# First columns in six pieces, routing products twice an iteration, low parts of the weights on VectorE, raw words through GpSimd's queue

## The chip, the cores and the metric

The kernel runs on one core of one Trainium2 chip. The metric is the device time of one execution in microseconds (us). Five engines work side by side in the core: TensorE (PE in the profile; its weight loads are PEld), VectorE (DVE), ScalarE (ACT), GpSimd (POOL) and SyncE (SP, which here only issues transfers). Each of them takes its own instructions strictly in order. Transfers are issued from the queues of SP or of GpSimd and carried out by 16 DMA engines.

## What is computed

Attention over keys and values that are averaged in groups of eight; its output goes through a mixture of experts, one expert per token; that output goes through a dense layer with a maximum of three products.

```python
def _attn_ref(q, k, v):                      # 8 x 8 x 576 x 64
    k_p = k.reshape(B, H, Sp, pool, D).mean(axis=3)      # pool = 8
    v_p = v.reshape(B, H, Sp, pool, D).mean(axis=3)
    scores = scale * np.matmul(q, k_p.transpose(0, 1, 3, 2))
    attn = np.exp(scores - np.max(scores, axis=-1, keepdims=True))
    attn = attn / (np.sum(attn, axis=-1, keepdims=True) + 1e-09)
    return np.matmul(attn, v_p)

def _moe_ref(x, expert_emb, tau, w1, w2):    # x: 4608 x 512, 8 experts, F = 1024
    logits = xn @ en.T / tau                 # x and expert_emb with rows of length 1
    expert_idx = np.argmax(logits, axis=1)
    gate_w = probs[np.arange(N), expert_idx] # softmax of the logits
    for e in range(E):
        mask = expert_idx == e
        h = np.maximum(x[mask] @ w1[e], 0.0)
        out[mask] = gate_w[mask, None] * (h @ w2[e])
    return out

def _moe2_ref(x, w1, w2, w3, w_out):         # d_ff = 768
    h = np.maximum(np.maximum(x @ w1, x @ w2), x @ w3)
    return h @ w_out
```

## The kernel before

**Attention** (0 to about 212 us) goes over 36 tiles of 128 tokens in a loop `for it in range(NT + 4)`. An iteration does the scores of tile it-1 (`stage_s`), the product with the values of tile it-3 (`stage_a`), the transposes of the queries of tile it (`stage_q`) and the output of tile it-4 (`stage_x`). Between these stand the jobs that prepare the keys and values of a later batch b, from the list that `prep_steps(b)` returns; the table `at_` says in which iteration each job is written. For the six batches b = 2 to 7 the jobs are: GpSimd adds the groups of eight (`pool_k2` and `pool_v`, lines 267 and 278); ScalarE copies the pooled keys a second time beside themselves (`dup_k`), and GpSimd spreads the values into a block form (`spread_v`, line 284); TensorE transposes the keys (`trans_k`, tile ptk), then the values by themselves (`trans_v`, tile ptv, line 307); at last `vdot` multiplies the transposed values with the experts' vectors.

**Routing** runs on VectorE in the gaps. A routine queues generators of small steps; `fill(n)` takes n of them. A step that needs TensorE stops its generator, and `boundary()` moves such a stop on by one state each time that it is called: in one call the products are written, in a later one the steps behind them are released. The attention loop calls `boundary()` once, at the top of an iteration. One chain of such steps ends in the list `idg`, which says which tokens the first items of the experts take.

**The experts** (212 to 728 us): 18 items of 256 tokens and 4 of 128. `run` goes through eight steps per item, four products with w1 (`mm1`, tile ph) and four with w2 (`mm2`, tile py). Two steps ahead, `split(i, piece)` takes a piece of the raw weights to a high part (ScalarE, tile whi) and a low part (tile wlo, line 1001): on GpSimd for odd pieces of items 0 to 4 (`i < NE`, with NE = 5) and for the very first, otherwise on VectorE. `gather` fetches an item's tokens by `idg` through GpSimd's queue (tile xrow, line 961) and `transpose_x` turns them (tile px). ScalarE and VectorE make high and low parts of the hidden values (tiles hhi and hlo).

`between` is called twice in each of the eight steps. It first serves the rest of the routing, and after that two generators. `conversions` turns 48 blocks of 64-bit words of the dense layer's weights into floats on VectorE: a block's raw words (tile cvraw, 256 KB, two buffers) are loaded two blocks ahead (line 1134, SP's queue), and a block takes five steps (lines 1150, 1163, 1166, 1168 with the next load, 1171). `combinations` makes sums of these weights and stores them (line 1210, tile wst to wdram, GpSimd's queue), and ends with `columns(0, 1)`: the first token columns of the dense layer are read back from memory (tile yr, line 1249, SP's queue) in four pieces of 192, each in the one buffer that there is. After the load of a piece it lets three calls of `between` pass, and then writes the sums and the high and low parts (`sums`, lines 1266 to 1278, steps of one piece). From item 17 on (`last_pairs`) `between` moves this generator on twice.

**The dense layer** (728 us to the end) multiplies by a scheme of seven products (line 1579).

The order on each engine is the order in which the code writes the instructions. No scheduler stands between.

Of the kernel before, what the change touches and what calls it, by code (L numbers as in the profile page):

```python
# [21 lines left out]
def attention_moe_moe_kernel(  # L22
# [27 lines left out]
    P = 128  # L50
# [65 lines left out]
    if True:  # L116
# [61 lines left out]
        if True:  # L178
# [69 lines left out]
            def prep_steps(b):  # L248
# [3 lines left out]
                vp = qp.tile([P, 5, D], F32, tag="vp", name=f"vp{b}")  # L252
# [22 lines left out]
                def pool_v(c0, c1, n):  # L275
                    for w in (4, 2, 1):
                        dst = vt[0:n, c0:c1, 0:w, :] if w > 1 else vp[0:n, c0:c1, :].unsqueeze(2)
                        nc.gpsimd.tensor_tensor(dst, vt[0:n, c0:c1, 0:w, :], vt[0:n, c0:c1, w : 2 * w, :], op=A.add)
# [12 lines left out]
                def trans_k(cs, h0, h1):  # L291
# [9 lines left out]
                    nc.scalar.copy(kb[D:P, h0:h1, 1, :], ps[D:P, 0:col].rearrange("p (h s) -> p h s", s=SP))  # L301

# [35 lines left out]
                if b == 1:  # L338
                    pk = [lambda: (pool_k(0), pool_k(1)), lambda: (pool_k(2), pool_k(3)), lambda: pool_k(4)]
                    pk += [lambda: (pool_v(0, 4, P), pool_v(4, 5, 64))]  # L340
                else:
                    pk = [lambda: (pool_k2(), pool_v(0, 4, P), pool_v(4, 5, 64))]
# [650 lines left out]
            def split(i, piece):  # L993
                src = w_raw(piece)
                if not (i >= NPAIR and piece < 4):
# [4 lines left out]
                    eng = nc.gpsimd if i < NE and piece % 2 or (i, piece) == (0, 0) else nc.vector  # L1000
# [115 lines left out]
            def conversions():  # L1116
# [61 lines left out]
            def combinations():  # L1178
# [49 lines left out]
                for _ in columns(0, 1):  # L1228
                    yield
# [6 lines left out]
            def columns(g, bufs):  # L1236
# [5 lines left out]
                w_ = HW // 2 if bufs == 1 else HW  # L1242
                rows = []
                for c in range(2):
                    for n in range(0, HW, w_):
                        t = tl["yr"].tile([P, 2, 2, w_], F32, tag="yr", name=f"yr{g}_{c}_{n}", bufs=bufs)
# [3 lines left out]
                        if bufs == 1:  # L1250
                            for _ in range(3):
                                yield
                            yield from sums(t, c, n, w_)
                        rows.append((t, c, n, w_))
                if bufs > 1:
                    yield
                    for a_ in rows:
                        yield from sums(*a_)
# [61 lines left out]
            def between(half, p_=0):  # L1320
# [7 lines left out]
                else:  # L1328
# [3 lines left out]
                    if last_pairs:  # L1332
                        next(cb, None)
# [94 lines left out]
            for b in range(1, B):  # L1428
                need = (b // 2) * 9 + (0 if b % 2 == 0 else 4)
                at_ = [need - 7, need - 3, need - 1, need, need, need + 1, need + 2]  # L1430
                at_ = {1: [2, 3, 3, 2, 3, 4, 4, 5, 6, 7], 2: [need - 5, need - 2] + at_[2:]}.get(b, at_)
# [9 lines left out]
            for it in range(NT + 4):  # L1441
# [16 lines left out]
                while kvnext < B and kvnext * 4.5 - 11 <= it:  # L1458
                    kv[kvnext] = (load_rows("kraw", k, kvnext, KC), load_rows("vraw", v, kvnext, RC))
# [70 lines left out]
    def second(st, groups, again=False):  # L1530
# [143 lines left out]
        ahead = columns(groups[0], 2) if again else iter(())  # L1674
        for g in groups:
# [5 lines left out]
            ahead = columns(g + 1, 2) if nxt else iter(())  # L1681
# [83 lines left out]
```

## Time and profile before

| what | value |
|---|---|
| three runs | 1281.42, 1281.93, 1282.61 us (median 1281.93) |
| profiled execution | 1281.78 us, its span 1279.9 us |
| TensorE busy | 1225.6 us, 96% of the span |
| VectorE busy | 802.7 us, 63% |
| ScalarE busy | 581.4 us, 45% |
| GpSimd busy | 346.5 us, 27% |

Busy shares are averages over stages with different limits. How a stage stands is read from the table by windows further down; "PEclk" there is the granted TensorE clock, of which 1.00 is the higher level. A row of a timeline gives the start, the duration, engine, line, operation, tiles and shape; a bracket says how long the engine was idle before it and for what. "x4" behind a row says that four instructions follow each other there.

### The profile page before, as it was taken

The page shows a single profiled execution, that of the slowest core. Times are in us where ns is not written, and L with a number is a line of the kernel's source. Part 1 is how long each engine was busy: PE and PEld are TensorE (multiplying, and loading weights), DVE is VectorE, ACT ScalarE, POOL GpSimd, SP SyncE. Part 2 cuts the span into 40 slices and gives each one's busy share as a digit, 9 for nine tenths or more (in the row PEclk, how much of TensorE's full clock was granted, in tenths as well). Part 3 has the DMA queues.
Part 4 walks back from the last instruction along what each step waited for, and adds up shares of the span by engine and source line. Part 5 has one row for each costly group of instructions (what it writes and reads, how often), then busy time and mean ns, then how long its engine had stood idle before and what let it go on. Part 6 is the DMA issues. An engine that isn't in the chain of part 4 may idle for free. (4 is left out here: it accounts for less than half of the span.)

```text
span 1279.9 us, 22372 instructions
## 1 busy us (share of the span) xinstructions
PE 1225.6 (96%) x8281; PEld 1164.2 (91%) x8281; DVE 802.7 (63%) x1551; ACT 581.4 (45%) x1040; POOL 346.5 (27%) x357
## 2 busy tenths in 40 slices
PE   4999998989899999999989999999999999999997
PEld 3888787989899999999979899899998998998995
DVE  6776784788789899899654446355256345345450
ACT  2566555435566666666535423333234223223231
POOL 7985643434500403223000300201302103103101
PEclk9899999999999999999999999999999999999999
DMA  9867335421885644953516768367376475664631
GB/s 261 252 202 214 121 113 206 150 82 35 232 286 199 217 147 161 292 175 132 190 50 229 265 238 304 115 248 280 119 266 231 165 253 209 210 240 181 226 146 52
DMA packets 100088, 246.21 MB, mean 192 GB/s; under 512 B 17102, under 2 KB 57084, under 8 KB 91908
## 3 DMA queue, kind: packets, MB, share of 16 engines
q1 hardware_dynamic: 90660, 201.67, 47.3%
q0 software_dynamic: 9312, 43.04, 9.5%
q8 instruction: 67, 1.10, 0.3%
q14 instruction: 49, 0.40, 0.1%
HBM read 252.23 MB, written 46.98 MB: 234 GB/s over the span
## 5 line engine op out<-in xcount | busy, mean ns | idle before, releaser
L1579 PE MATMUL p<-yhi,wt 128*128 128x384 f32 x1512 | 387.2, 336 | 0.7 <-ACT yo L1093 0.7
L1579 PEld LDWEIGHTS p<-yhi,wt 128*128 128x128 f32 x1512 | 273.5, 188 | 1.4 <-ACT yo L1093 0.9
L1579 PE MATMUL p<-ylo,wt 128*128 128x384 f32 x756 | 254.0, 336 | 0.0
L1587 ACT COPY s<-p 128x384 f32<-128x384 f32 x162 | 77.8, 480 | 222.2 <-PE p L1579 214.0
L1021 PE MATMUL ph<-xhi,whi 128*128 128x256 f32 x576 | 164.9, 286 | 8.0 <-DVE hlo L1037 8.0
L1069 PE MATMUL py<-hhi,wlo 128*128 128x256 f32 x576 | 164.0, 285 | 3.3 <-DVE wlo L1001 3.3
L1069 PE MATMUL py<-hhi,whi 128*128 128x256 f32 x576 | 165.4, 287 | 1.0 <-ACT whi L999 1.0
L1021 PE MATMUL ph<-xhi,wlo 128*128 128x256 f32 x576 | 163.8, 284 | 1.9 <-DVE wlo L1001 1.9
L1021 PE MATMUL ph<-xlo,whi 128*128 128x256 f32 x576 | 163.7, 284 | 1.2 <-DVE xlo L988 1.2
L1069 PE MATMUL py<-hlo,whi 128*128 128x256 f32 x576 | 163.5, 284 | 0.0
L1579 PEld LDWEIGHTS p<-ylo,wt 128*128 128x128 f32 x756 | 142.1, 188 | 0.5
L1608 DVE TENSOR_TENSOR blk<-p,s 128x384 f32<-128x384 f32 x108 | 59.7, 553 | 114.1 <-PE p L1579 113.9
L1564 POOL DMA_INDIRECT gt<-gbuf,ix x26 | 37.1, 1428 | 322.4 <-DMA ix<-idbuf 316.0
L1021 PEld LDWEIGHTS ph<-xhi,whi 128*128 128x128 f32 x576 | 111.0, 193 | 9.6 <-DVE hlo L1037 9.2
L1069 PEld LDWEIGHTS py<-hhi,wlo 128*128 128x128 f32 x576 | 111.0, 193 | 4.1 <-DVE wlo L1001 4.1
L1021 PEld LDWEIGHTS ph<-xhi,wlo 128*128 128x128 f32 x576 | 111.2, 193 | 2.3 <-DVE wlo L1001 2.3
L1021 PEld LDWEIGHTS ph<-xlo,whi 128*128 128x128 f32 x576 | 111.1, 193 | 1.4 <-DVE xlo L988 1.4
L1069 PEld LDWEIGHTS py<-hhi,whi 128*128 128x128 f32 x576 | 111.1, 193 | 1.2 <-ACT whi L999 1.2
L1069 PEld LDWEIGHTS py<-hlo,whi 128*128 128x128 f32 x576 | 111.2, 193 | 0.0
L1001 DVE TENSOR_TENSOR wlo<-w2raw,whi 128x1024 fp32r<-128x1024 f32 x78 | 94.8, 1221 | 9.5 <-ACT whi L999 9.5
L961 POOL DMA_INDIRECT xrow<-xbuf,idg x40 | 69.6, 1740 | 113.4 <-PE px L982 87.8
L999 ACT CAST whi<-w2raw 128x1024 fp32r<-128x1024 f32 x88 | 91.8, 1044 | 5.5 <-PE py L1069 3.9
(307 smaller groups left out, 2338.0 us busy)
## 6 DMA issues: line engine op xcount, KB each, us to landing
wt<-wdram SPq DMA_DIRECT2D x51, 1792.0 KB
w1raw<-in_moe_w_dram SPq DMA_DIRECT2D x88, 512.0 KB
w2raw<-in_moe_w_dram SPq DMA_DIRECT2D x88, 512.0 KB
wdram<-wst POOLq DMA_DIRECT2D x9, 1792.0 KB, 7.2
ybuf<-yo SPq DMA_DIRECT2D x40, 256.0 KB
cvraw<-in_moe_w_dram SPq DMA_DIRECT2D x36, 256.0 KB
vraw<-in_v_dram SPq DMA_DIRECT2D x8, 1024.0 KB
xbuf<-x SPq DMA_DIRECT2D x16, 512.0 KB
```

The source lines that it names most:

```text
L961: nc.gpsimd.indirect_dma_start(out=t[:, j, :], out_offset=None, in_=xbuf[0:nr, :], in_offset=bass.IndirectOffsetOnAxis(ap=idg[:, b_ : b_ + ...
L999: nc.scalar.copy(hi, src)
L1001: eng.tensor_tensor(lo, src, hi.bitcast(F32), op=A.subtract)
L1021: nc.tensor.matmul(ps[:, f, :], a_[:, c, fs], b_[:, c, :], start=(n == 0), stop=(n == 3 * DC - 1))
L1069: nc.tensor.matmul(py[:, c // 2, (c % 2) * 256 : (c % 2 + 1) * 256], a_[:, f, c * P : (c + 1) * P], b_[:, f, :], start=(piece == 0 and f = ...
L1564: nc.gpsimd.indirect_dma_start(out=gt[g][:, j : j + 1], out_offset=None, in_=gbuf[:, :], in_offset=bass.IndirectOffsetOnAxis(ap=cols[j], a ...
L1579: nc.tensor.matmul(ps, a_, b_, start=(start and c + n == 0), stop=(c == 1 and n == 2), skip_group_check=True)
L1587: nc.scalar.copy(t, ps)
L1608: tt(src, add[0], add[1], op=A.add)
```

## The change

1. For b = 2 to 7 the pooled values are written beside the pooled keys into one tile (`vp = kp[:, :, 1, :]`). `trans_kv` transposes both together, five transposes for a batch where there were ten; `dup_k` is left out, the ScalarE copies of a batch go from nine to eight, the key rows come in chunks of 128, and `vdot` is written one iteration earlier. `pool_k2` adds in six instructions instead of nine; the largest has 1024 elements a partition instead of 768.
2. The first addition of `pool_v` is written in two halves.
3. For b = 1 the five key reductions are written one per job.
4. From the time when the last chain before the experts is queued (`dense[0] == 2`) the attention loop calls `boundary()` a second time in each iteration.
5. Low parts go to GpSimd for odd pieces of items 0 and 1 alone. Twelve instructions move from GpSimd to VectorE.
6. The 48 loads of raw words are issued from GpSimd's queue.
7. `columns(0, ...)` works in six pieces of 128 with two buffers. The first two loads are written together, then eight calls of `between` pass before the first sums, and each later load stands behind the sums of the piece two before. `between` moves the generator on once.

```diff
-                vp = qp.tile([P, 5, D], F32, tag="vp", name=f"vp{b}")
+                vp = kp[:, :, 1, :] if b > 1 else qp.tile([P, 5, D], F32, tag="vp", name=f"vp{b}")
...
-                    for c0, c1, n in ((0, 3, P), (3, 4, KC[3]), (4, 5, KC[4])):
+                    for c0, c1, n in ((0, 4, P), (4, 5, RC[4])):
...
+                def trans_kv(cs, r0):
+
+                    ps = pq.tile([P, 512], F32, tag="pq", name=f"ptk{b}_{r0}")
+                    col = 0
+                    for c in cs:
+                        n = RC[c]
+                        nc.tensor.transpose(
+                            ps[:, col : col + n], kp[0:n, c].rearrange("p two d -> p (two d)"), ident[0:n, 0:n]
+                        )
+                        col += n
...
+                        nc.scalar.copy(kb[0:D, at_[0], 0, at_[1]], src)
+                        nc.scalar.copy(kb[D:P, at_[0], 1, at_[1]], src)
+                        a0 = a1
+                    nc.scalar.copy(vT.rearrange("p c r -> p (c r)")[:, r0 : r0 + col], ps[D:P, 0:col])
...
-                    eng = nc.gpsimd if i < NE and piece % 2 or (i, piece) == (0, 0) else nc.vector
+                    eng = nc.gpsimd if i < 2 and piece % 2 or (i, piece) == (0, 0) else nc.vector
...
-                        nc.sync.dma_start(raws[n].rearrange("p f t -> p (f t)"), rows[n][1].bitcast(I32))
+                        nc.gpsimd.dma_start(raws[n].rearrange("p f t -> p (f t)"), rows[n][1].bitcast(I32))
...
-                for _ in columns(0, 1):
+                for _ in columns(0, False):
...
+                load(0)
+                load(1)
+                for _ in range(1 if whole_ else 8):
                     yield
-                    for a_ in rows:
-                        yield from sums(*a_)
+                for k_ in range(len(at_)):
+                    yield from sums(*rows[k_])
+                    load(k_ + 2)
...
                     next(cb, None)
-                    if last_pairs:
-                        next(cb, None)
...
+                if dense[0] == 2 and it < NT:
+                    boundary()
```

On VectorE, at the end of the attention, the list `idg` is made between the steps of the tiles. psc and pav are the products of a tile (the number is the tile's), mx, sh and rs its steps, vi, v2, vn and va the steps that lead to `idg`. Before:

```order
L416 TENSOR_REDUCE mx34_2406<-psc34_2400 128x8
L627 COPY vi_1_2411<-p_early_2332 128x10
L419 TENSOR_TENSOR sh34_2413<-psc34_2400,mx34_2406 128x576
L516 TENSOR_SCALAR v2_1_2408<-vi_1_2411 128x10
L518 TENSOR_SCALAR vn_1_2409<-vi_1_2411 128x10
...
L521 SCALAR_TENSOR_TENSOR va_1_2410<-v2_1_2408,va_1_2410 128x10
L465 TENSOR_SCALAR rs31_2452<-pav31_2439 128x8
L518 TENSOR_SCALAR idg_82<-va_1_2410 128x10
```

The same engine and steps in the changed kernel:

```order
L451 TENSOR_REDUCE mx32_2249<-psc32_2243 128x8
L662 COPY vi_1_2254<-p_early_2194 128x10
L454 TENSOR_TENSOR sh32_2256<-psc32_2243,mx32_2249 128x576
L551 TENSOR_SCALAR v2_1_2251<-vi_1_2254 128x10
L553 TENSOR_SCALAR vn_1_2252<-vi_1_2254 128x10
...
L556 SCALAR_TENSOR_TENSOR va_1_2253<-v2_1_2251,va_1_2253 128x10
L500 TENSOR_SCALAR rs29_2289<-pav29_2282 128x8
L553 TENSOR_SCALAR idg_82<-va_1_2253 128x10
```

`idg` now stands at tile 29 of `pav` and tile 32 of `psc`, where it stood at tiles 31 and 34: two iterations earlier.

On GpSimd, from the gather of item 2 on (xrow; the number behind wlo is the piece), before:

```order
L961 DMA xrow_3015<-xbuf,idg 128x512 x2
L1001 TENSOR_TENSOR wlo_3_3023<-w1raw_105,whi_3_3022 128x1024
L1001 TENSOR_TENSOR wlo_5_3127<-w2raw_2513,whi_5_3126 128x1024
L1001 TENSOR_TENSOR wlo_7_3211<-w2raw_2515,whi_7_3210 128x1024
L1001 TENSOR_TENSOR wlo_1_3314<-w1raw_103,whi_1_3313 128x1024
L961 DMA xrow_3383<-xbuf,idg 128x512 x2
L1001 TENSOR_TENSOR wlo_3_3391<-w1raw_105,whi_3_3390 128x1024
L1001 TENSOR_TENSOR wlo_5_3510<-w2raw_2513,whi_5_3509 128x1024
```

The same queue from the same gather on in the changed kernel:

```order
L996 DMA xrow_2945<-xbuf,idg 128x512 x2
L1036 TENSOR_TENSOR wlo_3_2953<-w1raw_105,whi_3_2952 128x1024
L1036 TENSOR_TENSOR wlo_5_3057<-w2raw_2443,whi_5_3056 128x1024
L1036 TENSOR_TENSOR wlo_7_3141<-w2raw_2445,whi_7_3140 128x1024
L996 DMA xrow_3313<-xbuf,idg 128x512 x2
L996 DMA xrow_3697<-xbuf,idg 128x512 x2
L1169 DMA cvraw_3863<-in_moe_w_dram 128x512
L1169 DMA cvraw_3955<-in_moe_w_dram 128x512
```

The low parts end with item 1, and the loads of raw words stand behind the gathers.

On SP's queue, in item 17 (w1raw and w2raw are the weights of the item after it), the loads of the first columns before:

```order
L948 DMA w1raw_102<-in_moe_w_dram 128x4x256
L1249 DMA yr_0_0_8139<-ybuf 128x2x192 x2
...
L948 DMA w1raw_105<-in_moe_w_dram 128x4x256
...
L948 DMA w2raw_2512<-in_moe_w_dram 128x2x512
L1249 DMA yr_0_192_8301<-ybuf 128x2x192 x2
```

The same place in the changed kernel:

```order
L983 DMA w1raw_102<-in_moe_w_dram 128x4x256
L1287 DMA yr_0_0_8069<-ybuf 128x2x128 x2
L1287 DMA yr_0_128_8072<-ybuf 128x2x128 x2
...
L983 DMA w1raw_105<-in_moe_w_dram 128x4x256
...
L983 DMA w2raw_2444<-in_moe_w_dram 128x2x512
L1287 DMA yr_0_256_8326<-ybuf 128x2x128 x2
```

Two pieces are asked for at once, and the third stands two weight loads further back than the second did.

## Rows read from the trace of the kernel before

**Rows 1.** The page's second line: busy time of each engine, share, instructions.

```profile
PE 1225.6 (96%) x8281; PEld 1164.2 (91%) x8281; DVE 802.7 (63%) x1551; ACT 581.4 (45%) x1040; POOL 346.5 (27%) x357
```

**Rows 2.** Busy time by stage: window, length, five engines' busy time, PEclk, DMA share, GB/s.

```profile
20.00:200.00 180.00, 168.43 (x1243) 148.84 (x1242) 133.15 (x352) 103.28 (x263) 117.34 (x167) 0.97 0.61 186
200.00:212.00 12.00, 8.27 (x48) 7.28 (x46) 5.29 (x12) 7.29 (x14) 8.88 (x6) 0.86 0.77 247
...
262.00:345.00 83.00, 76.63 (x643) 75.16 (x644) 63.91 (x123) 37.98 (x54) 37.10 (x18) 0.98 0.40 107
345.00:600.00 255.00, 255.00 (x2136) 255.00 (x2135) 231.08 (x429) 167.01 (x243) 57.97 (x34) 1.00 0.63 209
600.00:668.00 68.00, 60.88 (x480) 59.11 (x480) 45.49 (x63) 36.37 (x55) 2.99 (x3) 0.97 0.34 110
```

**Rows 3.** PE's waits, 20 to 200 us: line, waited for: total us, times, longest.

```profile
PE psc L401 <- DVE sh L419: 4.9, 2, 2.7
```

**Rows 4.** The tile ptv: duration in ns, minimum, median, maximum.

```profile
L307 PEld LDWEIGHTS ptv<-ident,vp x40: 105/111/173, 24.1 to 183.2; 128*64 128x64 f32 x32, 64*64 64x64 f32 x8
```

**Rows 5.** Timeline of VectorE and GpSimd at 133 us.

```profile
132.71 3.38 DVE L512 TENSOR_TENSOR oh<-w,wm 128x72 f32<-128x72 f32 x1
...
134.21 2.88 POOL L267 TENSOR_TENSOR kraw<-kraw 128x768 f32<-128x768 f32 x2
```

**Rows 6.** Timeline at the end of the attention: VectorE, GpSimd, TensorE.

```profile
199.57 0.16 DVE L518 TENSOR_SCALAR idg<-va 128x10 int32<-128x10 f32 x1
...
200.02 1.16 POOL L961 DMA_INDIRECT xrow<-xbuf,idg  x1 [15.85 <-DVE rs L467]
...
206.34 0.33 PE L982 MATMUL px<-ident,xrow 128*128 128x128 f32 x1 [3.33 <-DMA xrow<-xbuf,idg]
```

**Rows 7.** PE's waits, 262 to 345 us.

```profile
PE ph L1021 <- DVE hlo L1037: 3.5, 2, 3.1
PE py L1069 <- DVE wlo L1001: 1.6, 1, 1.6
```

**Rows 8.** Line 1001 on GpSimd and on VectorE: duration in ns, minimum, median, maximum.

```profile
L1001 POOL TENSOR_TENSOR wlo<-w1raw,whi x11: 2350/2395/2986, 202.5 to 331.1; 128x1024 fp32r<-128x1024 f32 x11
...
L1001 DVE TENSOR_TENSOR wlo<-w2raw,whi x78: 1208/1219/1227, 223.4 to 721.9; 128x1024 fp32r<-128x1024 f32 x78
```

**Rows 9.** Timeline of SP, VectorE and GpSimd, 319 to 332 us.

```profile
319.46 0.35 SPq L1134 DMA_DIRECT2D cvraw<-in_moe_w_dram  x1
...
319.93 0.42 DVE L1168 SCALAR_TENSOR_TENSOR mraw<-cvraw,mraw 128x256 int32<-128x256 int32 x1
...
328.79 0.29 DVE L1150 TENSOR_SCALAR mraw<-cvraw 128x256 int32<-128x256 int32 x1 [7.98 <-DMA cvraw<-in_moe_w_dram]
...
331.27 2.53 DVE L1168 SCALAR_TENSOR_TENSOR mraw<-cvraw,mraw 128x256 int32<-128x256 int32 x1
...
331.13 2.39 POOL L1001 TENSOR_TENSOR wlo<-w1raw,whi 128x1024 fp32r<-128x1024 f32 x1 [5.48 <-ACT whi L999]
```

**Rows 10.** Waits, 600 to 668 us: of PE, and of VectorE.

```profile
PE ph L1021 <- DVE hlo L1037: 3.8, 3, 3.1
...
DVE ysum L1266 <- DMA yr<-ybuf: 10.2, 4, 2.8
```

**Rows 11.** Timeline of SP and VectorE at the third piece of the columns.

```profile
640.08 0.89 SPq L1249 DMA_DIRECT2D yr<-ybuf  x2
...
643.34 0.56 DVE L1266 TENSOR_TENSOR ysum<-yr 128x384 f32<-128x384 f32 x1 [2.35 <-DMA yr<-ybuf]
```

**Rows 12.** The tile cvraw: its first use in a block (VectorE); duration, first and last start.

```profile
L1150 DVE TENSOR_SCALAR mraw<-cvraw x48: 278/284/293, 311.4 to 596.5; 128x256 int32<-128x256 int32 x48
```

**Rows 13.** GpSimd's queue: the gathers' issue (ns), their landing (us), and the page's row of stores.

```profile
L961 POOL DMA_INDIRECT xrow<-xbuf,idg x40: 996/1112/4532, 200.0 to 682.2; - x40
...
DMA to landing us min/median/max: 3.7/7.0/9.2
...
wdram<-wst POOLq DMA_DIRECT2D x9, 1792.0 KB, 7.2
```

More of the change, by code (lines that the diff above doesn't have):

```diff
@@ L276, in pool_v @@
                     for w in (4, 2, 1):
-                        dst = vt[0:n, c0:c1, 0:w, :] if w > 1 else vp[0:n, c0:c1, :].unsqueeze(2)
-                        nc.gpsimd.tensor_tensor(dst, vt[0:n, c0:c1, 0:w, :], vt[0:n, c0:c1, w : 2 * w, :], op=A.add)
+                        for a0 in range(c0, c1, 2) if w == 4 else (c0,):
+                            a1 = min(a0 + 2, c1) if w == 4 else c1
+                            dst = vt[0:n, a0:a1, 0:w, :] if w > 1 else vp[0:n, a0:a1, :].unsqueeze(2)
+                            nc.gpsimd.tensor_tensor(
+                                dst, vt[0:n, a0:a1, 0:w, :], vt[0:n, a0:a1, w : 2 * w, :], op=A.add
+                            )
                 def spread_v():
@@ L338, in prep_steps @@
                 if b == 1:
-                    pk = [lambda: (pool_k(0), pool_k(1)), lambda: (pool_k(2), pool_k(3)), lambda: pool_k(4)]
+                    pk = [lambda c=c: pool_k(c) for c in range(5)]
                     pk += [lambda: (pool_v(0, 4, P), pool_v(4, 5, 64))]
                 else:
-                    pk = [lambda: (pool_k2(), pool_v(0, 4, P), pool_v(4, 5, 64))]
+                    return [
+                        lambda: (pool_k2(), pool_v(0, 4, P), pool_v(4, 5, 64)),
+                        spread_v,
+                        lambda: trans_kv(range(4), 0),
+                        lambda: trans_kv([4], 4 * P),
+                        vdot,
+                    ]
                 return pk + [
@@ L1234, in split_o, with columns, load @@
                 nc.vector.tensor_tensor(olo[:, f, :], mraw[3][:, f, :], ohi[:, f, :].bitcast(F32), op=A.subtract)
-            def columns(g, bufs):
-                w_ = HW // 2 if bufs == 1 else HW
+            def columns(g, whole_=True):
+                w_ = HW if whole_ else HW // 3
+                at_ = [(c, n) for c in range(2) for n in range(0, HW, w_)]
                 rows = []
-                for c in range(2):
-                    for n in range(0, HW, w_):
-                        t = tl["yr"].tile([P, 2, 2, w_], F32, tag="yr", name=f"yr{g}_{c}_{n}", bufs=bufs)
+                def load(k_):
+                    if k_ < len(at_):
+                        c, n = at_[k_]
+                        t = tl["yr"].tile([P, 2, 2, w_], F32, tag="yr", name=f"yr{g}_{c}_{n}", bufs=2)
                         src = ybuf[:, GW * g : GW * g + GW].rearrange("(i c p) (j n) -> c p i j n", i=2, c=2, j=2)
@@ L1249, in columns @@
                             nc.sync.dma_start(t[:, i], src[c, :, i, :, n : n + w_])
[L1250 to L1253, printed above, removed]
                         rows.append((t, c, n, w_))
-                if bufs > 1:
+                load(0)
+                load(1)
+                for _ in range(1 if whole_ else 8):
                     yield
-                    for a_ in rows:
-                        yield from sums(*a_)
+                for k_ in range(len(at_)):
+                    yield from sums(*rows[k_])
+                    load(k_ + 2)
             def sums(t, c, n, w_):
@@ L1458, in attention_moe_moe_kernel @@
                 while kvnext < B and kvnext * 4.5 - 11 <= it:
-                    kv[kvnext] = (load_rows("kraw", k, kvnext, KC), load_rows("vraw", v, kvnext, RC))
+                    kv[kvnext] = (load_rows("kraw", k, kvnext, KC if kvnext < 2 else RC), load_rows("vraw", v, kvnext, RC))
                     kvnext += 1
@@ L1673, in second @@
         tokens(groups[0])
-        ahead = columns(groups[0], 2) if again else iter(())
+        ahead = columns(groups[0]) if again else iter(())
         for g in groups:
@@ L1680, in second @@
             nxt = g + 1 in groups
-            ahead = columns(g + 1, 2) if nxt else iter(())
+            ahead = columns(g + 1) if nxt else iter(())
             next(ahead, None)
```

13 lines of the change are left out of this document (12 added, 1 removed).

## The prediction, as it was put down before the run

> **What bounds the kernel now.** I read the engines' busy time first [rows 1]: TensorE is busy for 1225.6 of a span of 1279.9 us, so it is the bound, and only two things can be won: the 54.3 us in which it stands idle, and matmuls that are dropped. The table by stages [rows 2] then says where the idle time lies. Between 345 and 600 us TensorE is busy for all of 255.00 us; nothing can be won there, only lost. The edits touch four other stretches: attention, 20 to 200 us (180 - 168.43 = 11.6 us idle), the passage to the experts, 200 to 212 (12 - 8.27 = 3.7), the first expert items, 262 to 345 (83 - 76.63 = 6.4), and the items around 17, 600 to 668 (68 - 60.88 = 7.1). Together that is 28.8 us.
>
> The same rows show a second price. PEclk is under 1.00 in just these four stretches, and 1.00 where TensorE never stops. I count what a mean granted clock of c costs in a stretch as its length times (1 - c), since the lower level gives half: 180 x 0.03 = 5.4 us, 12 x 0.14 = 1.7, 83 x 0.02 = 1.7, 68 x 0.03 = 2.0. A wait that goes takes its part of this with it. The rows of waits and the timelines [rows 3 to 11] say who is late in each place, and whether an edit reaches it.
>
> The sum is made against the profiled execution, 1281.78 us, which is 0.15 us under the median of the runs; I leave that difference out.
>
> **Attention (edits 1 to 3).** What is dropped for certain: of the 40 transposes of the tile ptv, five in each of eight batches, 30 go. Their weight loads stand back to back with the others at a median of 111 ns [rows 4], and I take that as the time of one on TensorE: 30 x 0.111 = 3.3 us. The ScalarE copies go from nine to eight a batch and `dup_k` leaves the chain; ScalarE is busy for 103 of 180 us [rows 2], so I count that at nothing. Should ScalarE be late somewhere, one copy fewer can only help.
>
> Then the waits. The largest is for VectorE's sh, 4.9 us in two waits [rows 3]. VectorE is late because GpSimd blocks it: an `oh` of 72 elements took 3.38 us at 132.71, and ended only near 136, in the gap between two large additions of GpSimd of which two took 2.88 us from 134.21 on [rows 5]. Cutting `pool_v`'s first addition in two doubles the gaps there; `pool_k2` goes the other way, since its largest instruction grows from 768 to 1024 elements, 4/3 of the time, but has three instructions fewer. Which steps of VectorE meet which addition is a matter of chance, and the whole order shifts when `vdot` and the routing's steps move. Up to the 11.6 us idle and the 5.4 us of clock can be at stake. I take 3.0 us, about a quarter of the idle time, since one of the two block sizes shrinks and the other grows; the range is from -3 (one more pair of waits like the pair for sh, less its share of the good) to 9 us (half of 11.6 + 5.4). The spread of batch 1's reductions belongs to this term.
>
> **The passage to the experts (edit 4).** `idg` is done at 199.57, the first gather is issued at 200.02, and the first transpose of its tokens starts at 206.34 after 3.33 us of waiting for xrow [rows 6]. The order puts `idg` two iterations earlier on VectorE. An iteration is 180 us / 34 = some 5.3 us, so the gather is issued near 189 and its tokens, after the median 7.0 us [rows 13], lie there some 7 us before TensorE reaches them. The wait goes, and with it the 1.7 us of clock: 3.7 + 1.7 = 5.4. What is late next is item 0's low parts on GpSimd and its raw weights, which come earlier too, as both hang on the same list; I keep 0.4 for them and take 5.0, range 2 (only the wait, with another one of 1.3 in its place) to 6. The second `boundary()` also puts the routing's small products and their steps earlier; the steps on VectorE are the same ones, and it is busy for 133 of 180 us [rows 2]. It adds a stop only if a product is asked for before VectorE has its operand; that is in the first rival.
>
> **First items (edit 5).** Two causes are in [rows 7 to 9]. First the block again: at 331.13 GpSimd starts a low part of 2.39 us, and VectorE's L1168, 0.42 us at 319.93, takes 2.53 us at 331.27. There are seven such places between 262 and 345; each sets VectorE back by about 2.1 us. Twelve low parts (items 2 to 4) leave GpSimd, where they took 2.35 to 2.40 us, and cost VectorE 1.22 us each [rows 8]: it gains some 7 x 2.1 = 14.7 us and takes on 12 x 1.22 = 14.6. At its 63.91 of 83 us it stays far from full. The wait of 1.6 us for wlo at 262 stays, because it comes from item 1's last piece on GpSimd. Second, the raw words: at 328.79 VectorE had stood for 7.98 us for words that SP had issued at 319.46, and the hlo behind it held TensorE for 3.1 us. In the changed kernel these loads leave SP's queue (edit 6) and stand in GpSimd's, which holds only gathers there. So of 6.4 + 1.7 = 8.1 us I keep 0.8 for the piece at 262 and 0.3 for new small waits, and take 7.0; range 4 (the stop at 328 stays) to 9.
>
> **The columns (edit 7).** VectorE stood for yr four times, 10.2 us in all, and the worst wait of TensorE, 3.1 us for hlo, lies behind one of them [rows 10]: the third piece is issued at 640.08 and used at 643.34, with VectorE idle for 2.35 us [rows 11]. Four pieces in one buffer are four such round trips. With two buffers and eight calls of `between` ahead of the first sums, a load has a whole piece's five steps, two or three of the eight steps of an item of 23 us, so over 6 us where 3.3 were needed. VectorE gets twelve more instructions of at most 0.56 us, the time of the 192-wide sum [rows 11], under 7 us against 68 - 45.49 = 22 idle. Of 7.1 + 2.0 = 9.1 us I take 7.0: the waits for wlo that have no part in this stay, and the pieces, six at one step per call where four took two, end later, among the single items. Range 4 (half stays) to 9.
>
> **Raw words through GpSimd's queue (edit 6), apart from the 328 stop.** The trace has no such load. From below: SP's queue gets emptier by 48 issues of 0.35 us [rows 9], worth at most the 0.5 us by which a weight load might be late. From above: 48 blocks take 596.5 - 311.4 us [rows 12], 6.07 us for each, and a load is issued in the fourth of a block's five steps and used in the first step two blocks on, seven steps or 8.5 us later. GpSimd's own transfers in this trace land after 7.0 us (median of 40 gathers) and 7.2 us (stores of 1792 KB), 9.2 at the worst [rows 13]. That is inside 8.5 but for the worst, so I take 0. The range is from a gain of 0.5 to a loss of 8, which is a landing of 9.9 us: 46 x (9.9 - 8.5) / 2 = 32, less the 255 - 231.08 = 24 us that VectorE stands idle between 345 and 600 [rows 2].
>
> The trace shows one gather whose issue took 4.52 us where the median is 1.11 [rows 13]. The Trainium skill, on its page "SBUF — State Buffer" (section "Who interferes with whom", and the warning under "SBUF: two separate sides"), says that a transfer issued from GpSimd's queue gets its descriptors written by GpSimd, which VectorE can lock out for the length of an instruction, and it advises SP's or ScalarE's queue. By that rule edit 6 is wrong, and the second rival is what it would do here; by the median landings of these rows it costs nothing.
>
> **The sum.** 3.3 + 3.0 + 5.0 + 7.0 + 7.0 + 0 = 25.3 us; 1281.8 - 25.3 = 1256.5 us.
>
> **The rivals.** *Waits form again (15%).* The transposes and the columns come as said, but the new order of the attention and of the passage meets other blocks, so that the second and third terms give nothing and edit 5 gives half: 3.3 + 3.5 + 7.0 = 13.8 us, 1268.0 us. For it: VectorE is delayed in attention by chance meetings [rows 5]. Against it: the wait for xrow has one plain cause.
>
> *Raw words late (5%), slower than before.* If GpSimd's queue lands them later than 8.5 us, each pair of blocks is stretched by the excess, and since VectorE works in order, the low parts that TensorE needs wait behind L1150. The loss is 46 x (L - 8.5) / 2 - 24 us and exceeds the 25.3 us won from L = 10.6 us on. A stretched issue of 4.52 us before a landing of 7.0 gives L = 11.5, a loss of 69 - 24 = 45 us, and 1301.5 us. Against it: all 40 gathers, of 7.0 us in the median, land within 9.2 us, VectorE being busy for nine tenths of that stage.
>
> *The change doesn't do what it says at the passage (10%).* `idg` comes early, but the tokens were not alone: item 0's raw weights or low parts hold TensorE as long. Then that term is 0, and the time is 1261.5 us.
>
> **How the numbers follow.** The forecast itself has 65%, the rivals 15, 5 and 10; 5% stay for a smaller net of several errors, near 1275 and up. The range is to hold 8 in 10. Upward it takes in the first and third rival, to 1269; downward it takes the better ends of attention and of the first items, 1256.5 - 6 - 2 - 2 = 1246.5, so 1247. About 0.2% (2.6 us) is what a measurement of this kernel can tell from no change. Slower by more than that: 4% (the second rival from L = 10.8 on). Within it: 3%. Faster: 93%.
>
> **What would show it.** In the profile after: 10 instructions on the tile ptv instead of 40; PE's wait for xrow gone and PEclk near 1.00 in the passage; no VectorE instruction of 2.5 us after item 1; no wait for cvraw over 1 us and landings under 8.5 us; VectorE's waits for yr near nothing, TensorE busy for over 66 of the 68 us that answer to 600 to 668. The stage from 345 to 600 stays at 255 us. The forecast is wrong if that stage grows, if attention doesn't shrink by the 3.3 us, or if TensorE's waits only change their names.

## The result, and the profile after

The changed kernel takes 1262.6 us (median of 4 runs, 1260.79 to 1265.53), the kernel before 1282.27 us in the same comparison (1281.42 to 1282.78): a ratio of 0.9849, with an interval of 0.9832 to 0.9867. That is 19.7 us less, where 25.3 us were forecast; the time lies inside the forecast range. The profiled execution took 1260.98 us, its span 1259.2 us.

Fixed points of the program, read from TensorE's timeline, show where the time went. Before, the first product of the experts, the transposes ahead of items 5 and 16, the dense layer's first product and the last one of all:

```profile
212.02 0.38 PE L1021 MATMUL ph<-xhi,whi 128*128 128x256 f32 x1
...
343.66 0.27 PE L982 MATMUL px<-ident,xrow 128*128 128x128 f32 x1
...
606.56 0.27 PE L982 MATMUL px<-ident,xrow 128*128 128x128 f32 x1
...
726.96 0.45 PE L1579 MATMUL p<-yhi,wt 128*128 128x384 f32 x1 [0.68 <-ACT yo L1093]
...
1271.25 0.40 PE L1655 MATMUL po<-mohi,glo 128*128 128x512 f32 x1
```

After, the same five points (the start is the first column):

```profile
205.50 0.38 PE L1056 MATMUL ph<-xhi,whi 128*128 128x256 f32 x1
...
329.61 0.27 PE L1017 MATMUL px<-ident,xrow 128*128 128x128 f32 x1
...
592.58 0.27 PE L1017 MATMUL px<-ident,xrow 128*128 128x128 f32 x1
...
701.33 0.41 PE L1617 MATMUL p<-yhi,wt 128*128 128x384 f32 x1
...
1245.59 0.40 PE L1693 MATMUL po<-mohi,glo 128*128 128x512 f32 x1
```

The lead grows from 6.5 us to 14.05, stays at 13.98 through the long middle stage, reaches 25.6 us at the dense layer and stays there to TensorE's last product: in sum, though not term by term, TensorE alone did what was forecast. The span, though, is only 20.7 us shorter. What follows TensorE's end grew from 8.3 us to 13.2, and the rows of GpSimd's closing instructions (duration in ns, minimum, median, maximum) say where. Before:

```profile
L1760 POOLq DRAIN  x3: 40/113/2774, 1276.3 to 1279.7; - x3
...
L1719 POOLq INC_SWDGE_SEM  x1: 850/850/850, 1275.5 to 1275.5; - x1
```

After:

```profile
L1798 POOLq DRAIN  x3: 46/109/6689, 1251.7 to 1258.9; - x3
...
L1757 POOLq INC_SWDGE_SEM  x1: 1810/1810/1810, 1249.9 to 1249.9; - x1
```

The longest DRAIN took 3.92 us more and the step ahead of it 0.96 us more: 4.9 us that no step of the prediction had looked at.

The table by stages after (columns as in [rows 2]; the stages are moved to the same places of the program, and answer to 20 to 200, 262 to 345, 345 to 600 and the first 56 us of 600 to 668):

```profile
20.00:200.00 180.00, 164.93 (x1213) 146.74 (x1212) 134.62 (x353) 102.73 (x257) 120.45 (x161) 0.96 0.64 197
...
253.00:331.00 78.00, 75.75 (x655) 74.69 (x654) 64.07 (x140) 40.29 (x56) 11.48 (x12) 1.00 0.43 107
331.00:586.00 255.00, 255.00 (x2135) 255.00 (x2135) 230.25 (x426) 167.07 (x243) 57.49 (x74) 1.00 0.63 211
586.00:642.00 56.00, 56.00 (x471) 56.00 (x470) 45.36 (x70) 36.41 (x60) 2.74 (x3) 1.00 0.43 133
```

The items around 17 have no idle time left, and the middle stage has kept its 255.00 us. In attention TensorE is busy for 3.5 us less than in [rows 2], but idle for as much more.

### The profile page after: what moved, and what is told of

The parts are those of the page before. It is cut to its first block, busy times and chain, and to the rows that moved or that the text cites. A ratio compares the mean times of both kernels' runs of the same rounds, so it can differ in the third digit from the quotient of the medians.

```text
span 1259.2 us, 22318 instructions
## 1 busy us (share of the span) xinstructions
PE 1215.6 (97%) x8251; PEld 1158.0 (92%) x8251; DVE 799.2 (63%) x1575; ACT 580.5 (46%) x1040; POOL 318.9 (25%) x383
## 5 line engine op out<-in xcount | busy, mean ns | idle before, releaser
L1036 DVE TENSOR_TENSOR wlo<-w2raw,whi 128x1024 fp32r<-128x1024 f32 x84 | 102.2, 1221 | 8.8 <-ACT whi L1034 8.7
L1036 DVE TENSOR_TENSOR wlo<-w1raw,whi 128x1024 fp32r<-128x1024 f32 x67 | 81.8, 1220 | 27.6 <-ACT whi L1034 26.5
```

The costliest lines, as they stand in the source:

```text
L1036: eng.tensor_tensor(lo, src, hi.bitcast(F32), op=A.subtract)
```

## The experiments

One table carries most verdicts. For each kernel it gives the start of the experts' first product, three stretches of TensorE's timeline (between the transposes ahead of the items named, and to the dense layer's first product), the time from TensorE's end to the end of the span, and the median. From the transposes of item 6 to those of item 16 every kernel takes 239.0 to 239.1 us, and the dense layer 544.6 to 544.7 us; they are left out. The medians come from five comparisons, in which the kernel before had 1280.5 to 1283.7 us, so one or two us between two rows of the last column are not read as an effect. The other columns are one trace for each row, and they scatter: in the eight traces whose attention is that of the changed kernel the first product comes between 203.3 and 207.8 us, and in the six whose items 3 to 6 are written as in it that stretch takes 72.8 to 77.0 us.

| kernel | first product | item 2 to 3 | item 3 to 6 | item 16 to dense | after TensorE's end | median us |
|---|---|---|---|---|---|---|
| before | 212.0 | 31.2 | 76.9 | 120.4 | 8.30 | 1282.3 |
| changed | 205.5 | 27.7 | 72.9 | 108.8 | 13.23 | 1262.6 |
| changed, again | 206.8 | 27.7 | 74.4 | 108.7 | 13.15 | 1264.1 |
| raw words on SP | 207.8 | 27.7 | 78.2 | 108.8 | 8.28 | 1265.2 |
| half of them | 204.7 | 27.7 | 79.0 | 109.1 | 10.73 | 1264.9 |
| each in two | 207.8 | 27.7 | 72.8 | 108.7 | 15.67 | 1264.8 |
| one boundary | 213.6 | 27.7 | 74.5 | 109.5 | 15.68 | 1273.7 |
| low parts to item 4 | 205.6 | 31.1 | 77.4 | 108.7 | 13.16 | 1268.6 |
| four pieces | 207.1 | 27.7 | 77.0 | 123.4 | 13.16 | 1277.7 |
| no halves | 205.1 | 27.7 | 73.8 | 109.0 | 13.62 | 1261.8 |
| transposes apart | 205.8 | 27.7 | 72.8 | 109.5 | 13.16 | 1262.0 |
| first 8 raw words | 203.3 | 27.7 | 74.3 | 109.2 | 9.10 | 1261.5 |
| first additions on VectorE | 217.1 | 27.7 | 75.7 | 108.9 | 9.10 | 1270.2 |

### What the closing stretch pays for

The changed kernel once more:

> The changed kernel once more, for a second trace. In its first trace TensorE ended 25.7 us earlier than before, but the span only 20.7 us, because the last stretch, from TensorE's end to the end of the span, was 13.2 us long instead of 8.3: GpSimd's closing DRAIN took 6.69 us where it took 2.77, and the step ahead of it 1.81 us where it took 0.85. Theory (the closing work grows with what was issued from GpSimd's queue): the same 13.2 us again, within 0.3. Rival (an accident of one execution): near 8.3 us, and the time near 1257. Attention's waits fall by chance: some of them stand elsewhere in this trace, by up to 2 us in all, if the runs' spread of 4.7 us comes from there.

Measured: 13.15 us, the DRAIN again 6.69 us. The closing stretch is a fixed price. The two traces differ in attention and in items 3 to 6, by 1.3 and 1.5 us; that the runs' spread of 4.7 us comes from there fits, but two traces don't show it. The time over the kernel before: 0.9834 (0.9806 to 0.9863).

```diff
-                        nc.gpsimd.dma_start(raws[n].rearrange("p f t -> p (f t)"), rows[n][1].bitcast(I32))
+                        nc.sync.dma_start(raws[n].rearrange("p f t -> p (f t)"), rows[n][1].bitcast(I32))
```

> The changed kernel with the 48 loads of raw words issued from SP's queue again. Theory (the closing work pays for GpSimd's transfers): the last stretch is back at 8.3 us, 4.9 less, the closing DRAIN near 2.8 us; the wait for raw words of some 8 us on VectorE may come back near 320 us and hold TensorE for up to 3.3 us; net 1.6 to 4.9 us faster than the changed kernel, 0.996 to 0.999 of it. Rival (the last stretch has another cause): it stays at 13.2 us, and the time is the same or up to 3.3 us longer.

Measured: 8.28 us, the DRAIN at its old 2774 ns. The 4.9 us belong to edit 6. VectorE's wait for raw words is 6.8 us, and TensorE's behind it 3.7 us; items 3 to 6 take 78.2 us, where the six traces named above lie between 72.8 and 77.0. The gain and the loss nearly cancel: a ratio of 0.9845 (0.9813 to 0.9876) beside the 0.9834 of the changed kernel on the same chip. The expected net gain didn't show.

```diff
+                        (nc.gpsimd if n % 2 else nc.sync).dma_start(...)
```

> Every second load of raw words from SP's queue, the others from GpSimd's: 24 of them instead of 48. If the closing work grows evenly with the transfers of GpSimd's queue, the closing DRAIN takes 2.77 + 3.92/2 = 4.7 us and the last stretch 10.8 us. If it depends on whether there are any at all, or on a limit that is passed, it stays at 13.2 or falls to 8.3.

Measured: 10.73 us, the DRAIN 4.73 us, as worked out for even growth.

```diff
+                        for p0_ in (0, 64):
+                            nc.gpsimd.dma_start(raws[n][p0_ : p0_ + 64]..., rows[n][1][p0_ : p0_ + 64]...)
```

> Each load of raw words as two transfers of 64 partitions on GpSimd's queue: 96 transfers instead of 48, the same bytes and rows. If the closing work is paid by transfer, the closing DRAIN takes 6.69 + 3.92 = 10.6 us and the last stretch some 18 us. If it is paid by bytes or rows, it stays at 13.2 us. The raw words' landing may get later, by the second issue; if VectorE then waits for them between 345 and 600 us, TensorE stays busy there all the same unless the waits exceed 24 us in sum.

Measured: 15.67 us. The longest DRAIN of this kernel and of the one with half of the words (ns, as above):

```profile
L1801 POOLq DRAIN  x3: 46/109/8567, 1254.3 to 1263.4; - x3
```

```profile
L1798 POOLq DRAIN  x3: 46/109/4729, 1256.7 to 1261.9; - x3
```

Both guesses were wrong: 48 more transfers with the same bytes add 1.88 us, not 3.92 and not 0. A transfer of 128 partitions adds 82 ns to the DRAIN (3.92 / 48), one of 64 partitions 60 ns (5.80 / 96). So the price goes partly by transfer and partly by size; bytes and rows, which are both halved here, are not told apart.

```diff
+                        (nc.gpsimd if n < 8 else nc.sync).dma_start(...)
```

> The changed kernel with only the first 8 of the 48 loads of raw words on GpSimd's queue, the other 40 on SP's. With all on SP's queue the closing stretch fell from 13.2 to 8.28 us, but the items around 320 us lost 1.5 to 5.3 us, since a load waited behind the transfers of SP's queue there; that place is in the first blocks. Theory (the two effects are separate): closing stretch 8.3 + 8 x 0.10 = 9.1 us, closing DRAIN near 3.4 us, and the items from the third to the seventh keep the 72.9 to 74.4 us of the changed kernel; some 4 us faster than it. Rival (SP's queue is late for other blocks too): these items or the stretch to 600 us lose 2 us or more, and the time is the same.

Measured: the closing stretch is 9.10 us and the DRAIN 3.42 us, as expected, and items 3 to 6 take 74.3 us. The profiled execution, 1256.88 us, is the shortest of the study, but the median of four runs is 1261.54 (ratio 0.9861, 0.9838 to 0.9885). The 4.1 us are in the trace; that the kernel is faster than the changed one is not shown, since the runs differ by more than that from attention.

### Undoing one part each

```diff
-                if dense[0] == 2 and it < NT:
-                    boundary()
```

> The changed kernel without the second call per iteration (edit 4 undone). Theory (the list of tokens was late by itself): TensorE waits again for xrow by 3 to 4 us before the first transpose of tokens, the clock falls there for some us, and the first product of the experts (near 205.5 to 208 us in the changed kernel, whose attention ends up to 2 us apart in two traces) starts 4 to 6 us later; all later stages keep their length. Time some 5 us over the changed kernel. Rival (weights or low parts are late as well): the first product starts at most 1.5 us later.

Measured: the first product comes at 213.6, 6.8 to 8.1 us later than in the two traces of the changed kernel (4 to 6 were expected), and the median is 11.1 us longer. The chain of causes in this kernel (VectorE's list, the gather, TensorE's wait):

```profile
200.00 0.16 DVE L553 TENSOR_SCALAR idg<-va 128x10 int32<-128x10 f32 x1
...
200.45 1.16 POOL L996 DMA_INDIRECT xrow<-xbuf,idg  x1 [14.79 <-DVE rs L502]
...
207.34 2.19 PE L1017 MATMUL px<-ident,xrow 128*128 128x128 f32 x8 [3.90 <-DMA xrow<-xbuf,idg]
```

In the changed kernel the same gather is issued 11.1 us earlier:

```profile
188.90 0.16 DVE L553 TENSOR_SCALAR idg<-va 128x10 int32<-128x10 f32 x1
...
189.34 1.16 POOL L996 DMA_INDIRECT xrow<-xbuf,idg  x1 [10.16 <-DVE rs L502]
```

The list was late by itself; the rival (weights or low parts late as well) falls. In this kernel's trace the closing stretch is 2.5 us longer at the same DRAIN of 6.69 us. The output's stores were late: each of the last ones waits for the landing of the one before, and the last is issued 3.57 us after TensorE's end (1256.38 us), where it is 1.05 us in every other kernel of the table:

```profile
1259.95 0.98 POOL L1698 DMA_INDIRECT out_dram<-ob,ix  x1 [2.81 <-DMA out_dram<-ob,ix]
```

Why these stores fell behind in this trace is not shown.

```diff
-                    eng = nc.gpsimd if i < 2 and piece % 2 or (i, piece) == (0, 0) else nc.vector
+                    eng = nc.gpsimd if i < NE and piece % 2 or (i, piece) == (0, 0) else nc.vector
```

> The changed kernel with odd low parts of items 0 to 4 on GpSimd again (edit 5 undone), the raw words still in GpSimd's queue. Theory (GpSimd's low parts block VectorE's instructions by some 2.1 us each): VectorE instructions of 2.5 us are back between 260 and 340 us, and TensorE loses 3 to 4 us there. Rival (the gain of 7.5 us in these items came from the raw words' queue alone): the items from the third to the seventh keep their length within 0.7 us.

Measured: items 2 to 3 take 31.1 us instead of 27.7, and items 3 to 6 take 77.4 instead of 72.9 to 74.4: 6.4 to 7.9 us in all, about twice what was expected. In the traces only the 3.4 us of items 2 to 3 stand clear of the scatter, since 77.4 is just beyond the 72.8 to 77.0 us named above; the median, 6.0 us longer, speaks for more. Instructions of VectorE that stand still are back, six between 277 and 337 us, of which these are three:

```profile
277.29 2.36 DVE L553 TENSOR_SCALAR idg<-va 128x34 int32<-128x34 f32 x1
...
307.70 2.90 DVE L1198 TENSOR_SCALAR cvy<-cvraw 128x256 int32<-128x256 int32 x1
...
326.97 2.37 DVE L1203 SCALAR_TENSOR_TENSOR mraw<-cvraw,mraw 128x256 int32<-128x256 int32 x1
```

Part of the extra is a wait of its own, 3.2 us of TensorE for a low part on GpSimd, whose queue now also holds the raw words. A load ahead of that low part stood there for 6.09 us, until VectorE was done with the buffer:

```profile
323.13 0.56 POOL L1169 DMA_DIRECT2D cvraw<-in_moe_w_dram  x1 [6.09 <-DVE mraw L1203]
...
326.69 2.36 POOL L1036 TENSOR_TENSOR wlo<-w1raw,whi 128x1024 fp32r<-128x1024 f32 x1
...
329.10 0.39 PE L1056 MATMUL ph<-xhi,wlo 128*128 128x256 f32 x1 [3.17 <-POOL wlo L1036]
```

```diff
-                for _ in columns(0, False):
+                for _ in columns(0, 1):
```

(with the function and the second step for `last_pairs` as before)

> The changed kernel with four pieces of 192, one buffer and two steps per call (edit 7 undone). Theory (each piece is a round trip that VectorE waits out): VectorE waits 10 us for yr, and from item 16's transposes to the dense layer TensorE loses 11 to 12 us against the changed kernel, as it did before. Rival (the earlier start of everything ahead makes the pieces harmless): under 4 us.

Measured: from item 16 to the dense layer 123.4 us, 14.6 more than the changed kernel and 3.0 more than before; where these 3.0 us come from is not shown. VectorE waits for yr as in [rows 10], and somewhat longer:

```profile
DVE ysum L1301 <- DMA yr<-ybuf: 12.5, 4, 3.7
```

In the changed kernel no such row is left. An earlier start of the work ahead doesn't help the round trips.

```diff
-                        for a0 in range(c0, c1, 2) if w == 4 else (c0,):
-                            a1 = min(a0 + 2, c1) if w == 4 else c1
+                        for a0 in (c0,):
+                            a1 = c1
```

> The changed kernel with the first addition of pool_v in one instruction of 1024 elements a partition (edit 2 undone). In the trace after, VectorE's `pre` at 137.08 took 2.62 us, as long as both halves together, so it was not let in between them. Theory (the halves open no gap): attention keeps its length within the 2 to 3 us by which it differs from one execution to the next, and the longest VectorE instructions of 72 elements stay between 2.5 and 4 us. Rival (the halves do open one): attention is 2 us or more longer than in every trace of the changed kernel, and instructions of 2.6 us and more become more.

Measured: the first product comes at 205.1 us, the time is 1261.8 us: no loss. The rows behind that expectation, from the changed kernel, with the GpSimd instruction that came just before the next two halves:

```profile
137.08 2.62 DVE L547 TENSOR_TENSOR pre<-pre 128x72 f32<-128x72 f32 x1
...
136.83 0.32 POOL L267 TENSOR_TENSOR kp<-kraw 64x64 f32<-64x64 f32 x1
137.10 1.27 POOL L280 TENSOR_TENSOR vraw<-vraw 128x512 f32<-128x512 f32 x1
```

The half is done at 138.4, but VectorE's step ends only at 139.7, after the second one. Edit 2 gave nothing that these runs show.

### What sets the pace of attention

> The changed kernel with keys and values of batches 2 to 7 pooled and transposed apart again (edit 1 undone, edits 2 and 3 kept). In the traces after, TensorE was busy for some 3 us less between 20 and 200 us, and idle for as much more. Theory (VectorE, blocked by GpSimd, sets the pace of the attention, not TensorE): the experts' first product comes within the 205 to 208 us of the changed kernel's traces, although 30 transposes are back. Rival (the 3.3 us were won, and new waits ate them): it comes 3 us or more later, near 209 to 211 us.

The edit puts the separate tile for the values, `dup_k`, `trans_k`, `trans_v` and their places in `at_` back for b = 2 to 7. Measured: the first product comes at 205.8 us, between the two traces of the changed kernel, and the time is 1262.0 us. TensorE does 30 more transposes and is no later, and 205.8 lies in the middle of the 203.3 to 207.8 us of the eight traces. Edit 1 as a whole won nothing that these runs show. That the transposes alone won nothing is argued: this kernel also has the smaller additions of `pool_k2` back, and VectorE's longest stop in attention is 3.4 us in it instead of 3.9.

> The changed kernel without the first two of the three additions of GpSimd for keys and values of batches 2 to 7; averages then go over two of eight rows, and the experts get other tokens, so that only the attention's length is to be read. It takes some 4.0 us of GpSimd's time from the keys and as much from the values of each of six batches, among them all instructions of over 1 us. Theory (VectorE's instructions stand still behind those additions): the VectorE instructions of 2.5 to 4 us after 60 us are gone, and the experts' first product comes 3 to 8 us earlier, near 200 us. Rival (the attention is paced by TensorE or by transfers): it stays within 2 us.

Measured, in one execution: the first product comes at 191.6 us, 13.9 us earlier than in the changed kernel, more than the expected 3 to 8, and TensorE is busy for most of attention (the window 20 to 200 us of this kernel, in which more of the work has moved):

```profile
20.00:200.00 180.00, 174.65 (x1320) 156.61 (x1319) 128.41 (x370) 111.04 (x277) 69.07 (x111) 0.99 0.68 215
```

No VectorE instruction of over 2 us is left after 60 us. GpSimd's additions, and not TensorE, set the pace of attention. That they do it by holding up VectorE fits the waits: between 20 and 200 us TensorE waits for VectorE for 9.8 us in the changed kernel and for 3.0 us here. But GpSimd's own way from the rows to the pooled keys gets shorter as well, and this run doesn't tell the two apart.

```diff
-                            nc.gpsimd.tensor_tensor(
+                            (nc.vector if w == 4 and b > 1 else nc.gpsimd).tensor_tensor(
```

(in `pool_v`, the same in `pool_k2`, on top of the kernel with 8 raw words on GpSimd's queue)

> The kernel with 8 loads of raw words on GpSimd's queue, and besides the first addition of keys and values of batches 2 to 7 on VectorE instead of GpSimd. Without the first two additions the experts' first product came 13.9 us earlier. Each first addition of 1024 elements takes 2.35 us on GpSimd and, by the low parts of the same size, 1.22 us on VectorE; with the small ones VectorE takes on 6 x 3.1 = 19 us between 20 and 200 us, of 135 busy now, and loses its stops of 2.5 to 4 us. Theory (the blocks set the pace, and VectorE has the room): no stop of over 2.6 us is left after 60 us, and the experts' first product comes 2 to 6 us before the 203.3 us of the version with 8 loads. Rival (VectorE's own work sets the pace, or it waits for the rows to land): the same or later.

Measured: the rival. The long instructions are gone, but the first product comes at 217.1 us, 13.8 later than in the kernel that it was made from, and the median is 1270.2 us (0.9885, 0.9847 to 0.9922). TensorE's largest wait in attention is now

```profile
PE psc L436 <- DVE rs L500: 14.0, 6, 2.8
```

six times up to 2.8 us, once for each of the six batches: a batch's additions all stand at one place in VectorE's order. For one batch:

```profile
76.64 1.54 DVE L267 TENSOR_TENSOR kraw<-kraw 128x1024 f32<-128x1024 f32 x2
78.11 2.68 DVE L280 TENSOR_TENSOR vraw<-vraw 128x512 f32<-128x512 f32 x3
80.72 0.74 DVE L451 TENSOR_REDUCE mx<-psc 128x8 f32<-128x576 f32 x1
```

That is 4.2 us where 3.1 were expected, as long as a block, and in each of six batches, while the changed kernel has three VectorE instructions of over 2 us after 60 us. The two runs together suggest that what counts is how often and how long VectorE is held up at one place, not by which engine. Additions spread over several iterations were not tried.

## Why the prediction was right, and where it wasn't

The terms, as they were put, beside what TensorE's timeline shows:

| term | forecast us | measured us |
|---|---|---|
| attention: 30 transposes | 3.3 | 0 |
| attention: waits | 3.0 | 1.0 |
| passage to the experts | 5.0 | 5.5 |
| first items | 7.0 | 7.5 |
| columns | 7.0 | 11.6 |
| raw words between 345 and 600 us | 0 | 0 |
| after TensorE's end | not seen | -4.9 |
| sum | 25.3 | 20.7 |

**Attention.** The step that failed is the first of the sum: 111 ns for each dropped transpose, "for certain". TensorE was busy for 168.43 of 180 us, and so taken as the bound there; but 9.5 of its 11.6 us of idle time were waits for VectorE, and these didn't shrink with the work: they are 9.8 and 11.2 us in the two traces of the changed kernel, and the first of these has a wait of 2.9 us for a load of queries besides. [rows 3] and [rows 5] held the answer, and the prediction used them for the second term alone. The last transposes of queries start at 194.33 us after and at 195.29 before: 1.0 us of the 6.3 forecast, and in the second trace they start 0.4 us later than before. So the prediction's own sign of being wrong, an attention that isn't shorter by 3.3 us, came true. The waits after stand at other places, most of them for VectorE still (TensorE's largest between 20 and 200 us):

```profile
PE pav L490 <- DVE dt L515: 4.6, 2, 3.2
PE pqT L411 <- DMA qgrp<-in_q_dram: 2.9, 1, 2.9
PE psc L436 <- DVE pre L547: 2.4, 1, 2.4
PE psc L436 <- DVE sh L454: 2.2, 1, 2.2
```

The claim that halves double the gaps was wrong; the claim that a larger `pool_k2` goes the other way may be right: in the changed kernel the `oh` of [rows 5] took 3.9 us, and with the keys pooled as before (transposes apart) 3.4. Of the rival in which waits form again, the half on attention came true and the half on the passage and items didn't. Edit 3 was not undone by itself.

The Trainium skill, "SBUF — State Buffer", section "Who interferes with whom", says that a VectorE instruction with two inputs in SBUF and a GpSimd instruction that reads SBUF exclude each other for the whole instruction. The 2.62 us of `pre` against its usual 0.22 agree with exclusion, but it lasted for two of GpSimd's instructions here, not one.

**The passage** came as put: the gather at 189.34 us (forecast near 189), no wait for xrow, PEclk 1.00. Undone, it costs 6.8 to 8.1 us. The third rival falls.

**First items.** The sum was right, 7.5 us in the first trace and 6.0 in the second for 7.0, and by two causes as put: undoing edit 5 gives back 3.4 us in items 2 to 3 and 6.0 us in the median, and with the raw words on SP's queue items 3 to 6 take 78.2 us again. (GpSimd's low parts of w1raw took up to 2.99 us in [rows 8], not 2.35 to 2.40; nothing hangs on it.) But the statement on the raw words was wrong: "no wait over 1 us, landings under 8.5". The load issued at 303.80 us was used at 315.36, after 11.6 us and a wait of VectorE:

```profile
303.80 0.58 POOL L1169 DMA_DIRECT2D cvraw<-in_moe_w_dram  x1 [44.34 <-DVE mraw L1203]
...
315.36 0.29 DVE L1185 TENSOR_SCALAR mraw<-cvraw 128x256 int32<-128x256 int32 x1 [3.32 <-DMA cvraw<-in_moe_w_dram]
```

That is the 11.5 us of the second rival, but in one block, not in all (four later ones wait for up to 1.8 us); TensorE did not wait for it in this trace, and by 1.4 us in the second one. The same block is late in every kernel but one, whichever queue it takes: VectorE's wait is 3.1 to 5.8 us through GpSimd's queue and 6.8 to 8.0 through SP's; with the transposes apart it is 0.6. The DMA engines are full there at hardly any rate, and the rows by queue (packets, MB, share) say with what:

```profile
304.00:308.00 4.00, 4.00 (x37) 4.00 (x36) 3.04 (x6) 1.83 (x3) 0.37 (x1) 1.00 1.03 21
```

```profile
q0 software_dynamic: 20, 0.08, 102.3%
q1 hardware_dynamic: 18, 0.00, 0.6%
```

In this window one load of raw words was issued, and 20 packets of GpSimd's queue take all of that share. The small transfers of the list gbuf, which SP issues beside it, take 0.6%, so they don't fill the engines; why the raw words' packets take so long stays open. The rule of the Trainium skill that was weighed against edit 6 (page "SBUF — State Buffer", section "SBUF: two separate sides") is stated there for VectorE's instructions of a two-port mode: while one runs, GpSimd can't write the descriptors of its transfers. If VectorE's instructions here are such, loads would be late in the middle stage, where VectorE is busiest. They are, by little: between 331 and 586 us VectorE waits for raw words in four blocks, 4.3 us in all,

```profile
DVE mraw L1185 <- DMA cvraw<-in_moe_w_dram: 2.5, 3, 1.2
DVE mraw L1185 <- DMA cvraw<-in_moe_w_out_dram: 1.8, 1, 1.8
```

where it is 0.2 us with SP's queue. Whether that rule is the cause is not shown; VectorE's own idle time took it up and TensorE stayed busy for all 255.00 us, so as a price of this change the rule isn't borne out. Edit 6 cost its time elsewhere, at the end.

**The columns.** The mechanism was right; the size was 11.6 for 7.0, and even the ceiling of 9.1 was too low. TensorE's idle time undercounts a stop. Around the longest one before, the products follow each other every 0.12 us though each counts as busy for 0.28:

```profile
645.28 0.28 PE L1021 MATMUL ph<-xlo,whi 128*128 128x256 f32 x1
645.40 0.28 PE L1021 MATMUL ph<-xhi,wlo 128*128 128x256 f32 x1
648.76 0.39 PE L1021 MATMUL ph<-xhi,whi 128*128 128x256 f32 x1 [3.08 <-DVE hlo L1037]
648.98 0.28 PE L1021 MATMUL ph<-xlo,whi 128*128 128x256 f32 x1
```

The row says 3.08 us, but from start to start it is 3.36 where 0.12 is normal, and the next step takes 0.22 instead of 0.12: 3.34 us lost, 0.26 more than the wait. With eight such stops between 600 and 668 us that is 2.1 us. The 0.7 us before the dense layer's first product is gone too: 9.1 + 2.1 + 0.7 = 11.9 (an estimate: the slower step behind a stop may be in the 2.0 us of clock already).

**After TensorE's end.** The prediction said how the span stands to the run, but took what follows TensorE's end as fixed. It priced edit 6 by landing times and by SP's issues; what a transfer on GpSimd's queue costs when the program closes was in no term. It cost 4.9 us.

That the time fell inside the range is in part luck: attention gave 5.3 us less than put and the close took 4.9, while the columns gave 4.6 more. 1262.6 us is also near the third rival's 1261.5, but that rival's cause was not there.

## What to carry to other kernels

Before work is taken off an engine, ask which wait ends last in that stage: an engine that is busy for 94% can still be paced by another one, and then the removed work comes back as idle time. Read the cost of a stop from start to start of the instructions around it, not from the idle time alone. And compare the stretch after the last computation too: transfers moved to GpSimd's queue can be paid for there.

## What the runs showed of the hardware

The closing DRAIN on GpSimd grows with what was issued from its queue: 2.77, 3.42, 4.73 and 6.69 us with 0, 8, 24 and 48 loads of 256 KB, which is 82 ns for each, and with the step ahead of it (0.85, 1.01, 1.33, 1.81 us) 102 ns. With 96 loads of 128 KB it was 8.57 us.

VectorE, shut out by GpSimd's additions, was not let in between the two halves of one addition: 2.62 us with halves, 2.47 us with a whole one, for a step that takes 0.22 us otherwise.
